# Batch 0's start rearranged and batch 2's attention moved three slots, in a banded-attention and low-rank mixer kernel

## Chip, cores, metric

One NeuronCore of a Trainium2 chip. The metric is the device time of one execution in microseconds (us), median of several. A profile's span (first to last instruction) is some 1.7 us shorter than the execution that it belongs to.

## The reference

```python
# attention: q, k, v are (8 batches, 8 heads, 576, 64), float32
scores = scale * q @ k.T                      # per batch and head
mask   = (0 <= i - j) & (i - j < 64)          # a band of 64
attn   = softmax(where(mask, scores, -1e9))
x      = (attn @ v) as (8, 576, 512)
# mixer
u   = x + (x.T @ U @ V).T                     # U (576, 32), V (32, 576)
out = u + relu(u @ w_ch1) @ w_ch2             # 512 -> 2048 -> 512
```

The 8 x 576 rows are worked on in nine chunks of 512 rows for the two large products. The attention of batch b+1 is slipped into the product of chunk b.

## The kernel before

A chunk is 32 slots. Slots 0 to 15 are each four matmuls of 512 columns and a relu (`ch1`), slots 16 to 31 four matmuls into the output (`ch2`). Pieces of the next batch's attention are put behind given slots:

```python
PLACE_2 = {                      # batch 2, inside chunk 1
    "S": [5, 5, 8, 8, 10],       # scores, exponential, mask
    "PV": [13, 13, 15, 15, 17],  # attention times V
    "TX": [12, 13, 14, 15, 16],  # DMA transposes of batch 3's K and Q
    "U": [19], "V": [21, 22, 23], "UT": [23, 24, 25, 26, 27],
}
```

Batch 0 has no product to hide in. It stands alone at the start, with matmuls whose result nobody reads (`unread`, `idle`) to keep TensorE busy. Its mask is added by a matmul of the identity with a bias (`masked`) instead of a product on DVE:

```python
def turn_over(n, cols=CH):                     # CH = 512
    for _ in range(n):
        nc.tensor.matmul(unread[:, 0:cols], idle[:, 0:P], idle[:, 0:cols], start=True, stop=True)

turn_over(9)
# ... masks ...
for what in ("K0", "K1", "Q0", "Q1", "S0", "S1", "K2", "K3", "Q2", "Q3", "S2", "S3"):
    # K, Q: 12 transposes into PSUM and a copy; S: bias matmuls, scores, exponential
    # ... cut ...
    turn_over({"K1": 3, "Q1": 1, "S0": 1, "K3": 1, "Q3": 1}.get(what, 0))
a["S"][HP]()                                   # the last block of all heads
# ... cut ...
for t in range(NT + 2):
    if t < NT:
        a["PV"][t]()                           # value tile t
    if 2 <= t < NFULL + 2:
        a["XT"][t - 2](); a["U"][t - 2]()
    elif t < 2:
        a["idle"](2)                           # two unread matmuls
for f in [a["U"][NT - 1]] + a["X3"] + a["HT"]:
    f()
# then chunk 0
```

All loads of K, Q, V and the weights stand in one queue of GpSimd, in this order: batch 0's K, Q, V, `w_ch1`, batch 1's K, Q, V, `w_ch2` in four parts, batch 2's K and Q. DMA transposes and the stores of the output stand in SyncE's.

The softmax here doesn't subtract the row's maximum and nothing guards it: scores larger than these inputs give would overflow.

## Time and profile before

| | |
|---|---|
| time | 330.74 us, median of 3 (330.69 to 330.99) |
| TensorE busy | 312.7 of 329.0 us |
| first product of chunk 0 | 26.39 us |
| PE waits at batch 2's scores | 2.67 us, until 73.67 |
| DMA engines busy (mean of 16) | 90% or more in slices 2 to 21 of 40, to 173 us |

In a timeline line the columns are start, length, engine, source line, operation, output and inputs, and in brackets how long the engine was idle before it and what ended that. "issue" means that no event of the program explains it.

### The profile page before, as it was taken

What the parts mean: (1) busy time and instruction counts of PE and PEld (TensorE: products, weight loads), DVE (VectorE), ACT (ScalarE), POOL (GpSimd) and SP (SyncE); (2) the same over time, 40 slices, a digit from 0 to 9 for tenths busy, and PEclk for the clock granted to TensorE, in tenths of its full rate; (3) what the DMA queues carried; (4) which work ended last, traced back from release to release, by engine and by line L of the source; (5) the groups of instructions that cost most, each with busy time, mean ns of one, the idle gap of its engine ahead of it and who ended that gap; (6) DMA issues with size and microseconds to landing.
All of it is one profiled execution on the core that took longest, in us unless ns stands there. A gap on an engine that the chain in (4) does not pass through costs nothing.

```text
span 329.0 us, 6715 instructions
## 1 busy us (share of the span) xinstructions
PE 312.7 (95%) x2790; PEld 147.0 (45%) x2790; DVE 171.2 (52%) x313; ACT 95.9 (29%) x150; POOL 103.0 (31%) x134
## 2 busy tenths in 40 slices
PE   6889999969999999899999999999999999999995
PEld 2544544534454444444444444444444444444442
DVE  4555486238645854476537653865387425114211
ACT  2515650317223330154016400640054001301400
POOL 8771778636537755407800400000000000000000
PEclk9979999999999999999999999999999999999999
DMA  8999999999999999999994796244200330021011
GB/s 114 156 220 197 161 193 166 124 173 173 138 147 211 166 143 146 187 181 149 157 175 101 103 119 176 54 89 104 90 26 2 79 99 32 0 82 48 0 66 64
DMA packets 151871, 39.56 MB, mean 120 GB/s; under 512 B 140960, under 2 KB 146080, under 8 KB 151840
## 3 DMA queue, kind: packets, MB, share of 16 engines
q0 software_dynamic: 100096, 18.36, 80.5%
q1 hardware_dynamic: 51744, 20.77, 35.0%
q8 instruction: 22, 0.36, 0.5%
q14 instruction: 9, 0.07, 0.1%
HBM read 37.14 MB, written 9.44 MB: 142 GB/s over the span
## 4 chain that ended last, share of the span: by engine, by line
PE 77%; DMA 9%; DVE 6%; ACT 5%; issue 1%; SPq 1%; POOL 0%; ACTq 0%; POOLq 0%
PE psA L583 32%; PE psU L605 32%; ACT pts L334 4%; PE xr L389 4%; DMA qf<-qn_110 2%; DMA uTc<-un 2%; DMA vA_104<-in_v_dram 2%; PE sc L315 2%; PE psv L506 2%; DMA qg<-in_q_dram 2%; DVE pts L336 2%; PE pshh L432 1%; DVE un L519 1%; PE uam L464 1%; SPq L284 1%
## 5 line engine op out<-in xcount | busy, mean ns | idle before, releaser
L583 PE MATMUL psA<-uTc,w1b 128*128 128x512 bf16 x576 | 132.0, 379 | 4.4 <-DMA uTc<-un 1.1
L583 PEld LDWEIGHTS <-w1b 128*128 128x128 bf16 x576 | 54.1, 98 | 68.3 <-issue 5.1
L614 DVE TENSOR_TENSOR osb<-psU,un 128x512 f32<-128x512 f32 x36 | 24.8, 690 | 79.3 <-PE psU L605 79.3
L334 ACT ACTIVATE pts<-sc 128x1024 bf16<-128x1024 f32 x32 | 31.4, 1028 | 7.7 <-PE sc L315 7.3
L336 DVE TENSOR_TENSOR pts<-pts,maskA 128x1024 bf16<-128x1024 bf16 x28 | 19.6, 703 | 11.4 <-ACT pts L334 11.4
L135 POOL DMA_DIRECT2D vA_105<-in_v_dram x16 | 14.1, 893 | 29.3 <-PE one L389 25.1
L519 DVE TENSOR_TENSOR un<-psv,xs_103 128x512 bf16<-128x512 f32 (+1 forms) x20 | 13.1, 686 | 11.7 <-PE psv L506 11.6
L519 DVE TENSOR_TENSOR un<-psv,xs_102 128x512 bf16<-128x512 f32 (+1 forms) x20 | 13.0, 684 | 11.0 <-PE psv L506 11.0
L135 POOL DMA_DIRECT2D vA_104<-in_v_dram x16 | 14.2, 894 | 14.0 <-PE xr L389 7.4
L126 POOL DMA_DIRECT2D qn_110<-in_q_dram x15 | 12.7, 847 | 10.8 <-DMA vA_105<-in_v_dram 4.7
L389 PEld LDWEIGHTS <-pts 128*64 128x64 bf16 x512 | 11.1, 113 | 10.7 <-issue 5.8
L126 POOL DMA_DIRECT2D kn_108<-in_k_dram x15 | 12.8, 851 | 9.5 <-DMA vA_105<-in_v_dram 5.2
L315 PEld LDWEIGHTS <-kf 64*64 64x64 bf16 x704 | 9.9, 107 | 10.9 <-issue 10.6
L126 POOL DMA_DIRECT2D kn_109<-in_k_dram x15 | 12.9, 860 | 5.9 <-DMA vA_104<-in_v_dram 3.7
L315 PE MATMUL sc<-qf,kf 64*64 64x128 bf16 (+1 forms) x576 | 11.3, 213 | 2.8 <-DMA qf<-qn_110 2.7
L126 POOL DMA_DIRECT2D qn_111<-in_q_dram x15 | 12.9, 859 | 3.1 <-DMA qn_111<-in_q_dram 1.3
L412 DVE TENSOR_TENSOR xs_102<-xr,rcp 128x512 bf16<-128x512 f32 (+1 forms) x18 | 12.4, 691 | 0.6
L506 PE MATMUL psv<-hh,vrep 128*128 128x512 bf16 x40 | 12.6, 379 | 0.0
L411 DVE RECIPROCAL rcp<-xr 128x8 f32<-128x8 f32 (+1 forms) x35 | 7.1, 202 | 10.3 <-PE xr L389 10.1
L412 DVE TENSOR_TENSOR xs_103<-xr,rcp 128x512 bf16<-128x512 f32 (+1 forms) x17 | 11.8, 692 | 0.6
L541 ACT COPY uTc<-tpu 128x512 bf16<-128x512 bf16 x9 | 5.3, 586 | 11.2 <-PE tpu L538 11.2
L389 PE MATMUL xr<-vA_104,pts 128*64 128x65 bf16 x160 | 6.6, 201 | 1.7 <-issue 1.4
(543 smaller groups left out, 514.7 us busy)
## 6 DMA issues: line engine op xcount, KB each, us to landing
out_dram<-osb SPq DMA_DIRECT2D x36, 256.0 KB, 4.1
vA_104<-in_v_dram POOLq DMA_DIRECT2D x16, 128.0 KB, 7.0
w1b<-in_moe_w_ch_dram POOLq DMA_DIRECT2D x2, 1024.0 KB, 16.0
vA_105<-in_v_dram POOLq DMA_DIRECT2D x16, 128.0 KB, 10.9
w2b<-in_moe_w_ch_dram POOLq DMA_DIRECT2D x4, 512.0 KB, 13.1
kn_108<-in_k_dram POOLq DMA_DIRECT2D x12, 128.0 KB, 11.8
qn_110<-in_q_dram POOLq DMA_DIRECT2D x12, 128.0 KB, 12.1
kn_109<-in_k_dram POOLq DMA_DIRECT2D x12, 128.0 KB, 8.6
```

The source lines that it names most:

```text
L126: nc.gpsimd.dma_start(out=dst[0:rows, t, :, :], in_=src[b, :, t * P : t * P + rows, :].rearrange("h p d -> p h d"),)
L135: nc.gpsimd.dma_start(out=va[:, t, :, 0:D], in_=v[b, :, t * P : (t + 1) * P, :].rearrange("h p d -> p h d"),)
L315: nc.tensor.matmul(sc[g][r0 : r0 + W, col * W : (col + n) * W], keys_of(j, u, rs), queries_of(j, blk, n, rs), start=not spare, stop=last o ...
L334: nc.scalar.activation(out=dst, in_=sc[:], func=ACT.Exp, scale=scale)
L336: nc.vector.tensor_tensor(out=dst, in0=dst, in1=maskA.rearrange("p g n w -> p g (n w)"), op=ALU.mult)
L389: nc.tensor.matmul(dst, pts[:, h // 2, h % 2, blk, :] if blk < NB - 1 else ptl[:, h // 2, h % 2, :], rhs, start=True, stop=True,)
L412: nc.vector.tensor_tensor(out=x[lo:hi, t, :, :].rearrange("p (a h) d -> p a h d", a=2), in0=xv[:, :, :, 0:D], in1=rcp[lo:hi].to_broadcast( ...
L506: nc.tensor.matmul(ps[0][:, n, :], vrep[:, off : off + P], hh["sb"][:], start=True, stop=True)
L519: nc.vector.tensor_tensor(out=u_tiles[g][rs, :], in0=ps[0][rs, n, :], in1=x[rs, t, :, :].rearrange("p h d -> p (h d)"), op=ALU.add,)
L583: nc.tensor.matmul(ps[:], w1b[:, dc, i * P : (i + 1) * P], uTc[:, :, dc, :], start=(dc == 0), stop=(dc == NDC - 1),)
L605: nc.tensor.matmul(acc[t][:], c1[i][:, t * P : (t + 1) * P], w2b[:, i, :], start=(i == 0), stop=(i == NFC - 1),)
L614: nc.vector.tensor_tensor(out=osb[:], in0=acc[t][:], in1=u_tiles[g][:], op=ALU.add)
```

## The change

Its intent is to shorten batch 0's start and to take the wait out of batch 2's scores. Five things are changed:

```diff
-turn_over(9)
+turn_over(56, 96)                                    # 56 unread matmuls of 96 columns
 # copies of K and Q of batch 0 out of PSUM
-copy = nc.vector.tensor_copy if spare and j >= HP // 2 else nc.scalar.copy      # K
+copy = nc.vector.tensor_copy if spare and j == 2 else nc.scalar.copy
-nc.vector.tensor_copy(out=place_of(qt, j), ...)                                 # Q
+copy = nc.scalar.copy if spare and j == 3 else nc.vector.tensor_copy
 # bias matmuls (B) are a piece of their own
-"K0 K1 Q0 Q1 S0 S1 K2 K3 Q2 Q3 S2 S3"
+"K0 K1 B0 B1 Q0 Q1 S0 S1 K2 K3 B2 Q2 B3 Q3 S2 S3 B4 S4"
-turn_over({"K1": 3, "Q1": 1, "S0": 1, "K3": 1, "Q3": 1}.get(what, 0))
+turn_over({"B1": 1, "Q1": 1, "S1": 1, "Q3": 1}.get(what, 0))
-        elif t < 2:
-            a["idle"](2)
+        elif t == 1:
+            a["idle"](1)
 PLACE_2
-    "S": [5, 5, 8, 8, 10], "PV": [13, 13, 15, 15, 17],
-    "U": [19], "V": [21, 22, 23], "UT": [23, 24, 25, 26, 27],
+    "S": [8, 8, 11, 11, 13], "PV": [16, 16, 18, 18, 20],
+    "U": [21], "V": [23, 24, 25], "UT": [25, 26, 27, 28, 29],
```

More of the change, by code (lines that the diff above doesn't have):

```diff
@@ L277, in f @@
             def f():
-                nc.vector.tensor_copy(out=place_of(qt, j), in_=tr(qb, j, b == 1))
+                copy = nc.scalar.copy if spare and j == 3 else nc.vector.tensor_copy
+                copy(out=place_of(qt, j), in_=tr(qb, j, b == 1))
             return f
@@ L302, in queries_of, with masked, SB @@
             return halves[rs, u0 : u0 + 2 * HP : 2 * HP - 1, :]
-        def masked(sc, bias):
+        sbank = {}
+        def masked(j):
+            sc = ps_big.tile([P, 2, CH], FP32, name="sc", tag="big")
             if spare:
+                bias, cols = maskB.rearrange("p n w -> p (n w)"), CH
+                if j == HP:
+                    bias, cols = maskB[:, 2:3, :].to_broadcast([P, HP, W]), HP * W
                 for g in range(2):
-                    nc.tensor.matmul(sc[:, g, :], ident[:], bias, start=True, stop=False)
+                    nc.tensor.matmul(sc[:, g, 0:cols], ident[:], bias, start=True, stop=False)
+            sbank[j] = sc
+        def SB(j):
+            return lambda: masked(j)
         def scores(sc, col, j, u, blk, n, last=False):
@@ L325, in f @@
             def f():
-                sc = ps_big.tile([P, 2, CH], FP32, name="sc", tag="big")
-                masked(sc, maskB.rearrange("p n w -> p (n w)"))
+                if j not in sbank:
+                    masked(j)
+                sc = sbank[j]
                 banks = [sc[:, g, :] for g in range(2)]
@@ L348, in SC8 @@
             else:
-                sc = ps_big.tile([P, 2, CH], FP32, name="sc8", tag="big")
+                if HP not in sbank:
+                    masked(HP)
+                sc = sbank[HP]
                 groups = [(sc, 0, 2)]
-                masked(sc[:, :, 0 : HP * W], maskB[:, 2:3, :].to_broadcast([P, HP, W]))
                 banks = [sc[:, g, :] for g in range(2)]
@@ L548, in attention @@
         pcs["S"] = [SC(j) for j in range(HP)]
+        pcs["B"] = [SB(j) for j in range(HP + 1)]
         pcs["S"].insert(0 if b >= NXU else HP, SC8)
@@ L641 @@
     PLACE_2 = {
-        "S": [5, 5, 8, 8, 10],
-        "PV": [13, 13, 15, 15, 17],
+        "S": [8, 8, 11, 11, 13],
+        "PV": [16, 16, 18, 18, 20],
         "TX": [12, 13, 14, 15, 16],
-        "U": [19],
-        "V": [21, 22, 23],
-        "UT": [23, 24, 25, 26, 27],
+        "U": [21],
+        "V": [23, 24, 25],
+        "UT": [25, 26, 27, 28, 29],
     }
@@ L684 @@
     )
-    for what in ("K0", "K1", "Q0", "Q1", "S0", "S1", "K2", "K3", "Q2", "Q3", "S2", "S3"):
+    order = "K0 K1 B0 B1 Q0 Q1 S0 S1 K2 K3 B2 Q2 B3 Q3 S2 S3 B4 S4"
+    for what in order.split():
         j = int(what[1])
-        if what[0] == "S":
-            a["S"][j]()
+        if what[0] in "SB":
+            a[what[0]][j]()
         else:
@@ L692 @@
             load_low_rank()
-        turn_over({"K1": 3, "Q1": 1, "S0": 1, "K3": 1, "Q3": 1}.get(what, 0))
-    a["S"][HP]()
+        turn_over({"B1": 1, "Q1": 1, "S1": 1, "Q3": 1}.get(what, 0))
     nc.vector.tensor_copy(out=maskA[:, 1, :, :], in_=maskA[:, 0, :, :])
```

## The prediction

> **What bounds the kernel now.** I read the page first. TensorE (PE) is busy 95% of the span, and in the forty slices it falls below 9 only in the first four slices and in slice nine. Each slice is 8.2 us.
>
> ```profile
> PE   6889999969999999899999999999999999999995
> PEclk9979999999999999999999999999999999999999
> ```
>
> From about 74 us to the end PE runs nearly without a break: listing every PE idle time with its cause gives only one wait of 1.1 us and pairs of 0.2 and 0.4 us per chunk. So the change, which touches only batch 0 and batch 2's slots, can win in two places: the first 26 us and the gap near 72 us. I then read the PE timeline of both.
>
> ```profile
> 68.82 1.89 PE L583 MATMUL psA<-uTc,w1b 128*128 128x512 bf16 x8
> 70.64 0.35 PE L315 MATMUL sc<-qf,kf 64*64 64x128 bf16 x12
> 73.67 0.50 PE L315 MATMUL sc<-qf,kf 64*64 64x128 bf16 x24 [2.67 <-DMA qf<-qn_110]
> ...
> 136.70 1.90 PE L583 MATMUL psA<-uTc,w1b 128*128 128x512 bf16 x8 [1.07 <-DMA uTc<-un]
> ```
>
> Batch 2's scores stand in slot 5, start at 70.64, run 12 matmuls on data that is there, and then PE waits 2.67 us for a transposed tile of Q which lands at 73.62. That is gap B.
>
> ```profile
> 14.94 0.38 PE L309 MATMUL sc_410<-maskB,ident 128*128 128x256 bf16 x2 [0.23 <-ACT pts L334]
> 15.25 0.32 PE L315 MATMUL sc_410<-qf,kf 64*64 64x64 bf16 x16
> 15.86 0.39 PE L389 MATMUL xr<-vA_104,pts 128*64 128x65 bf16 x13 [0.29 <-ACT pts L334]
> 17.65 0.23 PE L389 MATMUL xr<-vA_104,pts 128*64 128x65 bf16 x3 [1.41 <-issue]
> 17.81 1.02 PE L464 MATMUL uam<-idle 128*128 128x512 bf16 x2
> ...
> 26.39 1.02 PE L583 MATMUL psA<-uTc,w1b 128*128 128x512 bf16 x4 [0.45 <-DVE uTc L493]
> ```
>
> In the start (gap A) 13 of the 16 matmuls of the first value tile run, and then PE stands for 1.41 us with nothing in the program to wait for. The page's DMA part names an instruction queue with 22 packets and 0.36 MB, so 16 KB each; the trace's records of it put the first packet at 13.87 to 16.10 us, the second at 24.13 to 25.06. The stall falls at row 447 or 448 of PE's program, and 5,580 rows in 22 packets are 254 rows each. I take the stall for a late instruction block. The windows view shows what follows:
>
> ```profile
> 14.44:17.86 3.42, 1.49 (x53) 1.10 (x46) 0.06 (x1) 2.07 (x4) 2.95 (x5) 1.00 1.22 175
> 17.86:21.27 3.42, 3.42 (x41) 1.47 (x39) 2.03 (x6) 0.67 (x1) 3.42 (x5) 0.50 1.22 217
> ```
>
> The columns are length, then busy time of PE, PEld, DVE, ACT and POOL, then the granted clock. In a stretch with 1.49 of 3.42 us busy the clock was 1.00; in the next one it is 0.50.
>
> [...]the half-clock record is 3.413 us long, and 512-column matmuls start 0.43 us apart before 4.2 us and 0.216 after.[...]
>
> **The change, part by part.**
>
> *Batch 2's slots, 5 to 8, 8 to 11, 10 to 13.* Nothing is added. A slot is four 512-column matmuls at 0.216 us, so 0.86 us; three are 2.6 us of ready work put ahead of the wait. PE would reach the scores at 70.64 + 2.60 = 73.24, run its 12 ready matmuls (0.25) and wait from 73.49 to 73.62, were the rest unchanged. Gain about 2.5 us, less what an earlier start takes back below. At the new slots DVE has two V shifts (1.3 us), two mask products (0.69 each) and a relu after two exponentials of 1.03; with three buffers for the product I count the relu done about when PE wants the buffer, so at most 0.3 us is lost.
>
> *56 short matmuls for 9 long.* At half clock 96 columns take about 80 ns (half the speed of the 0.216 us per 512 warm); from 1.26 to 4.2 us some 37 run, the other 19 at 43 ns end at 5.1. K lands at 6.39 (first transposes at 6.43), so they delay nothing. What they do is to add 94 rows ahead: the listing of the order puts row 448 now in the middle of the fourth score block[...].
>
> *Bias matmuls ahead of Q.* Four of 0.216 and one filler replace three fillers: from 7.06 they end at 8.15 while Q landed at 7.88, so Q's transposes start 0.3 us later, Q0's copy ends at 9.5 instead of 9.17, the first exponential starts at 10.0 for 9.78. The second scores need no bias any more, so this is all it costs.
>
> *Copies of K3 and Q3 on ACT.* DVE did K2, K3, Q2, Q3 from 11.26 to 14.01 in a row; now K2 and Q2 end near 13.3, and ACT does K3 and Q3 between the exponentials, to about 14.0. The third exponential starts at 14.1 (13.87 before). No gain on the path; it is bound by Q2, whose data lands at 11.05 and whose copy is behind K2's.
>
> *Value tiles.* So the first of them starts at about 16.1 (15.86 before). But without the stall, at full clock, and with one filler of 0.22 for four that took 2.05 us, the five are paced by DVE: 0.21 + 0.69 with gaps 0.95 us each. DVE would be done at 16.5 + 5 x 0.95 = 21.3 instead of 24.01. From there to the first product took 2.4 us; chunk 0 would start at 23.7 instead of 26.39. Up to 2.7 us.
>
> *Sum and what is taken back.* 2.7 + 2.5 = 5.2 us if all comes through. But DMA runs full and most loads do not move with PE: the landings that the trace records are 23.22 for the first half of w1b, 34.69 for batch 1's Q (PE wanted it at 36.47, slack 1.78) and 49.65 for the last quarter of w2b (issued at 35.71, the longest of the four below; wanted at 51.29, slack 1.64).
>
> ```profile
> 34.98 1.48 POOL L225 DMA_DIRECT2D w2b<-in_moe_w_ch_dram  x2 [2.56 <-DMA qg<-in_q_dram]
> ...
> DMA to landing us min/median/max: 12.1/13.1/13.9
> ...
> 51.29 0.39 PE L605 MATMUL psU<-w2b,c_12_831 128*128 128x512 bf16 x1
> ```
>
> These loads are issued as earlier loads land (the bracket: an older load released this one), not as PE advances. So of the 2.7 at most about 1.6 passes 51 us, and with a block or a cold window left over perhaps 1.2; I count 1.4. At batch 2's scores PE then comes at 73.24 - 1.4 = 71.8, and the tile of Q, whose transposes start behind the first output store (53.09, which moves with PE), may come about 1 us earlier, at 72.6: the wait left is 72.6 - 72.05 = about 0.5 after the ready matmuls. Gap B gives 2.67 - 0.5, some 2.2. Behind that everything is PE's own pace: the wait of 1.07 at 136.70 follows from SyncE's row of transposes, which starts with PE, so I keep it. Sum 1.4 + 2.2 = 3.6; 330.74 - 3.6 = 327.1, of which I make 327.0.
>
> **The rivals.** *The start gives nothing.* The block stall moves into the scores and[...] comes again ahead of chunk 0: block 2 took its packet at 24.13, 6.5 us after row 448 was passed at 17.65[...]. Then only gap B is closed: about 328.2. *Everything passes.* If the loads move along with the earlier start, 2.7 + 2.5, and if the 1.07 at 136.70 goes too, 6.3: 324.5 to 325.5. The loads' latencies of 12 to 18 us on full queues speak against it. *The transposes become the bound again.* With batch 2 later in its chunk and PE 3.6 earlier, batch 3's transposed Q (landing at 99.25, wanted in slot 1 of the next chunk at 104.1) keeps 104.1 - 3.6 - 99.25 = 1.2 us; its issue starts when batch 2's fourth scores are done, at about the same time as before. If that is eaten, a wait of under 1 us comes back in chunk 2, and the wait at 136.70 can grow by as much: 328 to 329. *Slower:* for that ACT and DVE at slots 8 to 13 would have to stop PE for over 3 us; batches 3 to 7, with scores in slots 1 and 4, lose 0.6 us a chunk to the same conflict. I see no way to it.
>
> **Range and chances.** The first two rivals span 324.5 to 328.2, the third adds up to 1 us. The start carries most of the doubt (0 to 2.7), gap B less (1.5 to 2.7). Range 325.6 to 328.8. Over 2% faster means under 324.1, 6.6 us: more than both parts in full, so 4%. Slower by 2%: under 1%.
>
> **What would show it.** Right: no PE wait over 0.6 us at batch 2's scores; first product of chunk 0 between 23.5 and 25.2; clock 1.00 from 14 to 22 us; the "issue" gap gone from the value tiles, and found, if at all, in the fourth scores; waits of a few tenths at batch 1's Q or the last quarter of w2b near 50 us. Wrong: a half-clock record in the first 26 us, an issue gap of over 1 us ahead of chunk 0, a wait on DMA of over 1 us between 26 and 52 us or in chunk 2. The prediction fails upward if the loads issued in the first 20 us land earlier too, because then nothing takes the start's gain back.

## The result

327.44 us, median of 4 (326.82 to 329.19), against 330.87 (4 runs). The ratio is 0.9893, interval 0.9845 to 0.9941: faster by 1.1%, clear of noise, and inside the range predicted. A ratio here is the mean time of one kernel's fast runs over that of the other's of the same rounds, so it is not quite the ratio of the medians that are quoted.

From the page of the changed kernel, PE's busy tenths and the granted clock in 40 slices:

```profile
PE   7789899999999999899999999999999999999995
PEclk9999999999999999999999999999999999999999
```

The weak slice nine has gone, and so has the 7 in the clock's row. The PE timeline of the changed kernel at the places that the prediction showed for the one before:

```profile
14.76 0.36 PE L326 MATMUL sc<-qf,kf 64*64 64x128 bf16 x13 [0.31 <-issue]
15.23 0.38 PE L316 MATMUL sc<-maskB,ident 128*128 128x256 bf16 x2
15.54 0.32 PE L326 MATMUL sc<-qf,kf 64*64 64x64 bf16 x16
16.25 0.45 PE L402 MATMUL xr<-vA,pts 128*64 128x65 bf16 x16 [0.39 <-ACT pts L346]
...
23.54 1.02 PE L597 MATMUL psA<-uTc,w1b 128*128 128x512 bf16 x4 [0.45 <-DVE uTc L506]
...
35.06 0.45 PE L262 MATMUL tpw<-ident,qg 96*64 96x96 bf16 x12 [1.27 <-DMA qg<-in_q_dram]
...
72.19 0.50 PE L326 MATMUL sc<-qf,kf 64*64 64x128 bf16 x24 [0.25 <-DMA qf<-qn]
...
132.82 1.47 PE L597 MATMUL psA<-uTc,w1b 128*128 128x512 bf16 x6 [1.26 <-DMA uTc<-un]
```

All 16 matmuls of the first value tile run in one piece. The "issue" gap is in the fourth scores and 0.31 us long. Chunk 0 starts 2.85 us earlier, at 23.54. At 35.06 a wait of 1.27 us has come that was not there before: batch 1's Q lands at 35.01, where it landed at 34.69 before. At batch 2's scores 0.25 us of waiting is left of 2.67. The span is 325.1 us for 329.0. These 3.9 us divide as follows: 2.42 at batch 2's scores, 0.19 lost at the wait near 132 (1.26 for 1.07), and so some 1.65 won in the start: 2.85 at chunk 0, less the new wait of 1.27 and small differences. Up to the span's last us the trace records the granted clock in stretches: 13.65 us full, 3.41 half and 307.20 full in the kernel before, 317.44 full here. These are 4, 1, 90 and 93 times 3.413 us; a window here is that long, counted from the edge of a stretch. The windows view, in the columns of the prediction, for two windows of this run's clock; in the kernel before, the windows at this place began at 14.44 and 17.86, and the clock was half in the second:

```profile
13.56:16.97 3.41, 2.36 (x84) 1.73 (x86) 0.21 (x1) 3.30 (x5) 2.08 (x4) 1.00 1.73 170
16.97:20.38 3.41, 2.78 (x65) 1.92 (x60) 3.27 (x8) 0.62 (x1) 3.29 (x6) 1.00 1.21 228
```

PE is busy 2.36 us of 3.41 in the first (69%; 1.49 before, 44%), and the clock stays at 1.00.

### The profile page after: what moved, and what is told of

It is laid out like the page before. It is cut to its first block, busy times and chain, and to the rows that moved or that the text cites.

```text
span 325.1 us, 6773 instructions
## 1 busy us (share of the span) xinstructions
PE 309.4 (95%) x2806; PEld 149.9 (46%) x2831; DVE 169.7 (52%) x311; ACT 96.8 (30%) x152; POOL 104.1 (32%) x134
## 4 chain that ended last, share of the span: by engine, by line
PE 73%; DMA 12%; DVE 4%; ACT 4%; POOL 2%; SPq 2%; issue 1%; POOLq 0%; ACTq 0%
PE psU L619 33%; PE psA L597 30%; DMA qg<-in_q_dram 5%; ACT pts L346 3%; PE xr L402 3%; DMA vA<-in_v_dram 3%; DMA uTc<-un 3%; PE sc L326 2%; DMA qf<-qn 2%; PE psv L519 2%; SPq L285 1%; DVE pts L348 1%; PE pshh L445 1%; DVE c L606 1%; DVE un L532 1%
## 5 line engine op out<-in xcount | busy, mean ns | idle before, releaser
L619 PE MATMUL psU<-w2b,c 128*128 128x512 bf16 x556 | 130.4, 379 | 1.2 <-issue 0.2
L608 ACT ACTIVATE c<-psA 128x512 bf16<-128x512 f32 x75 | 44.7, 598 | 167.8 <-PE psA L597 167.8
L619 PEld LDWEIGHTS <-c 128*128 128x128 bf16 x576 | 54.9, 98 | 65.8 <-issue 3.0
L606 DVE TENSOR_SCALAR c<-psA 128x512 bf16<-128x512 f32 x69 | 46.0, 686 | 20.7 <-PE psA L597 20.0
L135 POOL DMA_DIRECT2D vA<-in_v_dram x32 | 28.5, 898 | 25.6 <-PE one L402 12.9
L532 DVE TENSOR_TENSOR un<-psv,xs 128x512 bf16<-128x512 f32 (+1 forms) x40 | 25.9, 684 | 20.6 <-PE psv L519 20.4
L126 POOL DMA_DIRECT2D kn<-in_k_dram x30 | 25.9, 864 | 26.1 <-DMA vA<-in_v_dram 14.2
L126 POOL DMA_DIRECT2D qn<-in_q_dram x30 | 25.3, 845 | 13.8 <-DMA vA<-in_v_dram 5.7
L425 DVE TENSOR_TENSOR xs<-xr,rcp 128x512 bf16<-128x512 f32 (+1 forms) x35 | 24.2, 691 | 1.2
L402 PE MATMUL xr<-vA,pts 128*64 128x65 bf16 x296 | 12.2, 196 | 0.6 <-ACT pts L346 0.4
```

Of the source, the lines that this page charges most:

```text
L126: nc.gpsimd.dma_start(out=dst[0:rows, t, :, :], in_=src[b, :, t * P : t * P + rows, :].rearrange("h p d -> p h d"),)
L135: nc.gpsimd.dma_start(out=va[:, t, :, 0:D], in_=v[b, :, t * P : (t + 1) * P, :].rearrange("h p d -> p h d"),)
L402: nc.tensor.matmul(dst, pts[:, h // 2, h % 2, blk, :] if blk < NB - 1 else ptl[:, h // 2, h % 2, :], rhs, start=True, stop=True,)
L425: nc.vector.tensor_tensor(out=x[lo:hi, t, :, :].rearrange("p (a h) d -> p a h d", a=2), in0=xv[:, :, :, 0:D], in1=rcp[lo:hi].to_broadcast( ...
L532: nc.vector.tensor_tensor(out=u_tiles[g][rs, :], in0=ps[0][rs, n, :], in1=x[rs, t, :, :].rearrange("p h d -> p (h d)"), op=ALU.add,)
L606: nc.vector.tensor_relu(out=c1[i][:], in_=ps[:])
```

## The experiments

Twelve kernels ran, in three series of four. Each series has its own 11 runs of the kernel before beside it; the first two series ran on one chip, the third on another. All results were correct. One run of after_again, 332.30, counts as slow (over 1.5% above its fastest) and is left out of its ratio. "chunk 0" is the start of its first product in the profiled run, and the two waits are PE's at batch 2's scores and at the chunk that starts near 132 to 139 us.

| kernel | median us (lowest to highest) | before | ratio (95%) | chunk 0 | wait, batch 2 | wait near 132 |
|---|---|---|---|---|---|---|
| e1_slots_only | 328.33 (326.02 to 328.96) | 332.03 | 0.9873 (0.9834 to 0.9912) | 27.87 | 0.34 | none |
| e2_start_only | 332.00 (331.53 to 335.05) | 332.03 | 1.0004 (0.9961 to 1.0047) | 23.80 | 0.71 + 2.49 | 1.90 |
| e3_long_fillers | 328.09 (326.54 to 329.14) | 332.03 | 0.9870 (0.9829 to 0.9911) | 26.86 | 0.21 | 0.64 |
| e4_late_start | 326.35 (325.47 to 328.05) | 332.03 | 0.9825 (0.9788 to 0.9863) | 25.09 | none | 0.28 |
| after_again | 327.27 (326.85 to 332.30) | 331.61 | 0.9865 (0.9839 to 0.9892) | 23.54 | 0.17 | 1.34 |
| e9_eleven_long | 329.39 (328.27 to 332.25) | 331.61 | 0.9941 (0.9904 to 0.9977) | 27.70 | none | 1.53 |
| e10_tiny_fillers | 328.65 (327.25 to 329.76) | 331.61 | 0.9907 (0.9875 to 0.9939) | 25.15 | none | 2.54 |
| e5_fill_and_slots | 326.52 (326.16 to 327.05) | 331.61 | 0.9844 (0.9817 to 0.9871) | 24.37 | 0.94 | 0.52 |
| e6_copies_back | 327.14, one run | 331.35 | - | 23.55 | 0.81 | 0.9 |
| e7_bias_back | 327.21, one run | 331.35 | - | 23.88 | 0.81 | 0.6 |
| e8_late_masks | 324.91 (323.57 to 327.66) | 331.35 | 0.9813 (0.9771 to 0.9855) | 23.85 | 1.00 | 1.85 |
| e11_masks_and_ut | 322.62 (322.23 to 324.66) | 331.35 | 0.9745 (0.9712 to 0.9779) | 23.84 | 1.77 | 0.60 |

The kernel before spreads far more than its first three runs showed: 329.55 to 334.06 over the first two series. The granted clock says part of why. One window of 3.41 us at half clock lowers a run's mean clock by 0.5 x 3.41 / 330 = 0.005, and of its 33 runs 18 have 0.990 or less, so the worth of two such windows or more (the half clock at the very end of a span counts too: the profile shown for the kernel before has one window and 0.5 us of that, and 0.994). Those take 332.8 us on average in the first series, against 331.1 for the others; 332.7 against 331.2 in the second; 332.1 against 330.9 in the third. Runs at 0.995 and more still spread from 329.55 to 332.11, so the clock is not all of it. A single profile shows only one draw.

### Slots alone

```diff
 # kernel before, and only:
-    "S": [5, 5, 8, 8, 10],  ...
+    "S": [8, 8, 11, 11, 13], ...          # the whole new PLACE_2
```

> Kernel before with batch 2's slots alone. Theory (the slots close gap B by themselves, the start is separate): chunk 0's first product at 26.4 us as before, wait at batch 2's scores 0.1 to 0.4 us instead of 2.67, no new PE wait over 0.3 us in slots 8 to 20, time 2.3 to 2.6 us under before, 328.2 to 328.5. Rival (the later slots make ACT and DVE stop PE): waits on DVE or ACT of over 0.5 us in chunk 1, gain under 1.8 us.

The wait shrank to 0.34 us and none came in slots 8 to 20, as the theory had it. But the median fell by 3.7 us, not by 2.3 to 2.6: in the medians the slots alone are worth as much as the whole change (0.9873, against 0.9893 and 0.9865 for the changed kernel). In its profiled run 2.33 us of the wait are gone, and the wait near 132 too (1.07 before), against a start that is 1.48 us later; what made the rest of the median's fall is not shown. This profiled run had a slower start, as its PE timeline tells:

```profile
6.23 0.69 PE L262 MATMUL tpg<-ident,kg 96*64 96x96 bf16 x12 [0.95 <-DMA kg<-in_k_dram]
...
19.22 0.23 PE L389 MATMUL xr<-vA,pts 128*64 128x65 bf16 x3 [1.56 <-issue]
...
75.06 0.50 PE L315 MATMUL sc<-qf,kf 64*64 64x128 bf16 x24 [0.34 <-DMA qf<-qn]
```

The 12 transposes took 0.69 us where the kernel before's profile has 0.45: half clock. The trace's clock record is full only from 10.17 us here, and half again from 20.41 to 23.82. The start thus differs between the two profiled runs, by 1.48 us at chunk 0, with the same instructions.

### Start alone

```diff
 # kernel after, and only PLACE_2 as it was:
-    "S": [8, 8, 11, 11, 13], ...
+    "S": [5, 5, 8, 8, 10],  ...
```

> Kernel after with batch 2's old slots. Theory (the landing of the transposed Q tile sets the pace, and moves only about as far as the first output store does): chunk 0 at 23.5, wait at batch 1's Q about 1.3, wait at batch 2's scores again 2.4 to 2.9, tile landing near 72.1, time about 1.5 us under before, 329.3. Rival A (the start passes in full): 2.8 us under before, 328.0. Rival B (the tile does not move at all, the start is worth nothing): wait over 4 us, 330.8.

The tile landed at 72.5 us, 1.1 earlier than in the profile on record, and the wait was 3.2 us in two parts, somewhat over what the theory said (2.4 to 2.9). The time said otherwise: 332.00 against 332.03, nothing gained. Its PE timeline, the window of its clock with the wait and the one behind it, and two later ones that are taken up below:

```profile
69.83 0.25 PE L326 MATMUL sc<-qf,kf 64*64 64x128 bf16 x4 [0.71 <-DMA qf<-qn]
72.57 0.50 PE L326 MATMUL sc<-qf,kf 64*64 64x128 bf16 x24 [2.49 <-DMA qf<-qn]
73.00 4.45 PE L597 MATMUL psA<-uTc,w1b 128*128 128x512 bf16 x12
```

```profile
70.06:73.48 3.42, 0.93 (x30) 0.61 (x27) 0.00 (x0) 0.60 (x1) 1.44 (x3) 1.00 1.69 198
73.48:76.89 3.41, 3.41 (x10) 1.21 (x9) 2.66 (x4) 1.34 (x2) 0.99 (x2) 0.50 1.63 198
134.92:138.33 3.41, 1.51 (x8) 0.51 (x6) 1.95 (x3) 0.00 (x0) 0.69 (x1) 1.00 1.49 196
138.33:141.75 3.42, 3.42 (x65) 1.73 (x64) 1.12 (x2) 2.02 (x4) 0.68 (x1) 1.00 1.58 222
```

PE was busy 0.93 of 3.42 us, and the clock then went to half for 3.41 us: twelve products took 4.45 us where the same twelve behind the wait of the kernel before took 2.76. So here the wait cost its length and, in the half-clock window behind it, 1.7 us more. Against the profile of the kernel before the sum closes: 1.10 us earlier behind the wait, 1.69 lost at half clock, 0.83 more at the next wait on DMA (1.90 for 1.07) make 1.42 us more, and the spans are 330.4 and 329.0. Whether the earlier start has a part in the clock's fall is not shown. Neither rival A nor the theory's 329.3 held. Of rival B it held that the start is worth nothing here, but the tile did move.

The last two window lines are a warning: PE was busy for 1.51 us, about as little as the 1.49 of the window from 14.44 us in the kernel before, and here the clock stayed full. In these two the busy time alone does not tell whether the clock falls.

### A later start on purpose

```diff
 # kernel after, and:
+    a["idle"](6)                          # 24 unread matmuls of 128 columns, 1.3 us
     for f in [a["U"][NT - 1]] + a["X3"] + a["HT"]:
         f()
```

> Kernel after with 24 more idle matmuls of 128 columns (1.3 us at full clock) ahead of the last part of batch 0, same result. Theory (loads that do not move with PE take back 1.3 us at batch 1's Q): chunk 0 at 24.8, the wait at batch 1's Q gone or under 0.2, time within 0.3 us of after. Rival (the start counts in full): 1.3 us slower than after.

```profile
25.09 1.02 PE L597 MATMUL psA<-uTc,w1b 128*128 128x512 bf16 x4 [0.44 <-DVE uTc L506]
...
34.90 0.45 PE L262 MATMUL tpg<-ident,kg 96*64 96x96 bf16 x12
35.18 0.42 PE L262 MATMUL tpw<-ident,qg 96*64 96x96 bf16 x12
...
71.67 0.65 PE L326 MATMUL sc<-qf,kf 64*64 64x128 bf16 x36
```

Chunk 0 starts 1.55 us later than in the changed kernel; K and Q of batch 1 are transposed with no wait between them, as Q has landed (at 34.90; at 35.01 in the changed kernel); and the time is 326.35, not over that of the changed kernel on the same chip in the next series (327.27). The last 1.3 us that the start wins are worth nothing: the rival that counts them in full would be at a ratio of some 0.990, and the interval ends at 0.986. In the traces Q lands at 34.61 in e1, with chunk 0 at 27.87, and at 35.01 in the changed kernel, with chunk 0 at 23.54: this load does not move with PE. That e4 came out 0.9 us lower fits the wait near 132 us, 0.28 for 1.34 in the profiled runs. Against e1, the slots alone in the same series, it is 2.0 us lower.

### What the 56 short matmuls do: rows or columns

Three kernels differ from the changed one in the first fillers alone.

```diff
-turn_over(56, 96)
+turn_over(9)                              # e3: as before, 4608 columns, 94 rows fewer
+turn_over(10); turn_over(1, 256)          # e9: the same 5376 columns, 90 rows fewer
+turn_over(56, 32)                         # e10: the same rows, a third of the columns
```

> Kernel after with the 9 long fillers of before, so 94 rows fewer ahead of everything. Theory (a late instruction block stalls PE at row 448, wherever that row stands, and loads take back what the start wins beyond 1.3 us): the issue gap comes back in the second value tile, 0.7 to 1.5 us long, chunk 0 at 24.2 to 25, wait at batch 1's Q shrinks to 0 to 0.6, time within 0.4 us of after; if the clock falls to half behind the gap, up to 1 us more. Rival (the stall is not tied to the row but to the first value tile or its data): a gap at the first value tile again. Rival (the start counts in full): about 1.2 us slower than after.

> Kernel after with 10 fillers of 512 columns and one of 256: the same 5376 columns as 56 of 96, but 90 rows fewer. It parts the two things that the short fillers do. Theory (rows move the late instruction block, columns keep PE busy up to K): fillers end near 5.8 us, clock full by 7 us in all or nearly all executions, but the issue gap of 0.7 to 1.5 us back at the second value tile and with it, in some executions, a half-clock window near 18 to 21 us; chunk 0 at 24.3 to 26; time 0 to 0.8 us over after. Rival (only the length matters): no gap, chunk 0 at 23.5.

> Kernel after with 56 fillers of 32 columns: the same rows as after, a third of the columns. Theory: fillers end near 3 us, PE idle 3 us before K[...] and the transposes and first scores run at half clock; the issue gap stays in the fourth scores, under 0.6 us; chunk 0 at 24.3 to 25.5; time 0 to 0.8 us over after since batch 1's Q takes back up to 1.3 us. Rival (only the rows matter): as after, 23.5.

The unaltered kernel ran beside e9 and e10 as their yardstick.

> The changed kernel unaltered, as the yardstick on this chip. By the runs so far: 326.4 to 327.5, one in four or five executions about 1.7 us slower[...].

It gave 327.27 us, one of six runs at 332.30 with a mean clock of 0.985. The PE timelines of e3 and of e9 at the gap:

```profile
19.16 0.19 PE L402 MATMUL xr<-vB,pts 128*64 128x65 bf16 x1 [1.22 <-issue]
```

```profile
18.68 0.22 PE L402 MATMUL xr<-vA,pts 128*64 128x65 bf16 x2 [1.47 <-issue]
```

In e3 the gap stands ahead of the first matmul of the second value tile, in e9 ahead of the 15th of the first tile (the expectation named the second tile; counting the rows, of which each matmul has two, its weight load and itself, gives the 15th of the first: 4 rows, so two matmuls, ahead of e3's). Both are row 448 of PE's weight loads and matmuls in order of time. So are the gaps of the kernel before, of e1, of the changed kernel, e2, e4 and e8, and, shown below, of e5 and e7 (445 to 448, as some records are missing). In these ten kernels it is the row and not the work that fixes the place. The 16 KB packet of the instruction queue ends 1.3 to 2.0 us ahead of the resumption in these traces (for instance 16.10 and 17.65 in the kernel before; 17.85 and 19.16 in e3; 12.93 and 14.76 in the changed kernel). In e10 PE comes to that row only at 15.9, 2.5 us behind the packet's end (13.45), and there is no gap. That the packet is what PE waits for is inferred from this; no record says so. e3's chunk 0 at 26.86 missed its 24.2 to 25: the clock was full only from 9.45 us, and half again from 19.69 to 23.10, behind the gap.

The windows view of e9 shows what follows the gap, and that of e10, whose gap stays hidden, something else further on:

```profile
15.73:19.14 3.41, 1.50 (x51) 1.13 (x50) 0.20 (x1) 1.71 (x4) 2.73 (x5) 1.00 1.17 228
19.14:22.55 3.41, 3.08 (x41) 1.68 (x40) 2.65 (x8) 0.67 (x1) 3.41 (x5) 0.50 1.24 218
22.55:25.97 3.42, 3.42 (x23) 1.61 (x22) 1.53 (x3) 0.18 (x1) 1.75 (x3) 0.50 1.20 215
```

```profile
131.45:134.87 3.42, 0.88 (x6) 0.41 (x5) 2.04 (x3) 0.00 (x0) 1.42 (x2) 1.00 1.54 187
134.87:138.28 3.41, 3.41 (x58) 1.65 (x57) 1.11 (x2) 1.71 (x4) 1.20 (x2) 0.50 1.40 269
```

In e9 the clock was full from 5.49 us, as was expected (by 7 us), but behind the window of the gap, with 1.50 us busy, it was half for two windows: chunk 0 at 27.70, 329.39 us. All six of its runs have mean clocks of 0.985 to 0.990. In e10 there is no issue gap of note, but PE stood idle for 3.46 us ahead of K, the clock was full only from 11.99 us, and chunk 0 came at 25.15; 328.65 us. So in the start both halves of "many" and "short" work: the rows move the gap into the fourth scores, where it is 0.31 us long (1.22 in e3, 1.47 in e9), the columns keep PE busy until K lands (its wait for K is 0.33 us, for 3.46 in e10). What of this reaches the end differs. The same stop of PE near 104 us, in the unaltered kernel, in e9 and in e10:

```profile
104.10 2.75 PE L597 MATMUL psA<-uTc,w1b 128*128 128x512 bf16 x12 [0.18 <-DVE c L606]
```

```profile
106.37 0.59 PE L597 MATMUL psA<-uTc,w1b 128*128 128x512 bf16 x2 [0.18 <-DVE c L606]
```

```profile
104.07 2.75 PE L597 MATMUL psA<-uTc,w1b 128*128 128x512 bf16 x12 [0.18 <-DVE c L606]
```

e9 is 2.27 us behind there and 2.45 at the end, so losing the rows costs time. e10 is not behind at all: its later start has been taken up, as in e4. Its profiled run lost its 2.7 us (span 327.8 for 325.1) near 134 us, where PE waited 2.54 us for 1.34 and the clock then went to half once. Its median is 1.4 us over the unaltered kernel's, over the 0 to 0.8 expected as e9's 2.1 is, but that the missing columns are the cause is not shown.

### Fillers and slots without the rest

```diff
 # kernel before, and only:
-turn_over(9)
+turn_over(56, 96)
+# and the new PLACE_2; bias matmuls, copies, idle turns as before
```

> Kernel before with the 56 short fillers and batch 2's new slots only; bias matmuls, copies and idle turns as before. Theory (those other parts do not reach the end, batch 1's Q takes back what they win): issue gap in the fourth scores, chunk 0 at 23.9 to 24.6, wait at batch 1's Q 0.3 to 0.9, time within 0.4 us of after. Rival (bias and copies are worth something): 0.7 us or more over after.

```profile
15.29 0.42 PE L315 MATMUL sc<-qf,kf 64*64 64x64 bf16 x16 [0.62 <-issue]
...
24.37 1.02 PE L583 MATMUL psA<-uTc,w1b 128*128 128x512 bf16 x4 [0.44 <-DVE uTc L493]
35.39 0.45 PE L262 MATMUL tpw<-ident,qg 96*64 96x96 bf16 x12 [0.77 <-DMA qg<-in_q_dram]
```

326.52 us, 0.75 under the changed kernel beside it, where within 0.4 was expected. The other parts of the change win nothing at the end, and this has the lowest median of the versions that contain only parts of the change. In the profiled runs it is 1.03 us behind the unaltered kernel near 104 us, and the next wait on DMA, 0.52 for 1.34, gives 0.82 of that back.

```diff
 # e6: kernel after, copies of K3 and Q3 back on DVE
 # e7: kernel after, each bias pair back beside its scores, 3 fillers ahead of Q
```

> Kernel after with the copies of K3 and Q3 back on DVE; one look, for the start only. Theory (the third exponential is bound by Q2's copy, which is behind K2's on DVE, so moving K3 and Q3 to ACT wins little): third exponential starts at 14.0 to 14.8 (14.16 in after), chunk 0 within 0.8 us of 23.5, wait at batch 1's Q takes the difference. Rival (the copies are what wins the start): chunk 0 at 24.8 or later.

> Kernel after with each bias pair back beside its scores, fillers ahead of Q again 3; one look, for the start only. Theory (the bias matmuls ahead of Q cost 0.3 us at the first exponential and are worth nothing later): first exponential near 9.8 (10.04 in after), chunk 0 within 0.5 us of 23.5. Rival (bias early is what wins the start): chunk 0 at 24.3 or later.

In e6 the third exponential started at 13.87 (14.16 in the changed kernel) and PE was through with batch 0 early enough to wait 0.85 us at 23.55 for the first half of `w_ch1`: with the copies back the start is not slower, and it meets the landing of the weights. In e7 the first exponential began at 9.64 (10.04), the gap was 0.74 us, chunk 0 at 23.88. Both as the theory said; one run each, 327.14 and 327.21.

### What else the page offered

The waits of the changed kernel name ten stops of PE for relus on DVE, 2.9 us in all, in batches 3 to 7. This is no part of the change.

```diff
 # e8: DVE's mask products of batches 3 to 7 become pieces of their own
+    "M": [3, 3, 3, 6, 6],                 # scores and exponentials stay in [1, 1, 1, 4, 4]
 # e11: e8, and one tile of batch 3's u, the third, transposed by TensorE
-                if b >= NXU:
+                if b >= NXU and not (b == NXU and t == 2):
                     nc.sync.dma_start_transpose(out=dst, in_=u_tiles[g][:])
+    PLACE_3 = {**PLACE, "UT": [18, 18, 22, 19, 20]}
```

> Not a test of the prediction but of the 0.6 us a chunk that the page shows for batches 3 to 7: kernel after with DVE's mask products of batches 3 to 7 issued two slots after their scores instead of ahead of the next relus. If PE waits there because DVE, in order, holds a relu behind a product that waits for an exponential, the ten waits on DVE's relus (2.9 us) go and the time falls by 2.3 to 2.9, to 324.4 to 325. Rival (the waits are the throughput of DVE): they move to another slot, time within 0.5 us of after.

> The kernel of late masks with one of batch 3's transposes of u, the last one that the next chunk waits for, done by TensorE (four matmuls, 0.22 us) instead of by DMA. If the PE wait of 0.3 to 2.5 us near 132 us is that transfer's landing, it is gone and the time falls by another 0.6 to 1.3 us against late masks alone, with a narrower spread: 323.3 to 324.2. Rival (another tile's landing takes its place): wait of over 0.5 us there, time as late masks alone.

All PE waits from 100 us on that the view lists, of the changed kernel and then of e8:

```profile
PE psA L597 <- DVE c L606: 2.9, 10, 0.4
PE psA L597 <- DMA uTc<-un: 1.3, 1, 1.3
```

```profile
PE psA L610 <- DMA uTc<-un: 1.9, 1, 1.9
```

The ten stops, 2.9 us, are gone: it was the order on DVE, where a relu stood behind a product that waited for an exponential, not DVE's throughput. e8 ran at 324.91, e11 at 322.62. The wait near 132 fell to 0.60 in e11 and did not vanish, so another tile's landing is next, as the rival had it, though not its time; the range of its runs was 2.4 us, and the gain of 2.3 over e8 is more than that wait can explain, so what e11's part is worth alone is not settled. Against the kernel before e11 is at 0.9745 and is the fastest that ran.

## Why the prediction was right

*Where the time could come from.* It named two places, the start and the wait at batch 2's scores. Those are the two places in which the traces differ. Right. It misread the page in one point: slice 17 is an 8 as well, and it holds the wait of 1.07 at 136.70, which later decided much.

*Gap B closes.* It said that 2.6 us of ready work covers the wait and that 0.5 is left, the tile landing at 72.6. Measured 0.25, and 72.15. Right, and so is the term "Gap B gives 2.67 - 0.5, some 2.2" for the two profiles: 2.42. In the medians the slots alone gave 3.7 us, in a series in which the kernel before ran at 332.03. What the prediction left out is a half clock behind such a wait. In e2's trace it is there, for 3.41 us, and cost 1.7 us more; that the kernel before has the same thing in many of its runs is inferred from their mean clock, not from a trace.

*The start.* Chunk 0 at 23.7 was said, 23.54 measured. The first value tile at 16.1: 16.25. DVE done with the tiles at 21.3: 21.16. Full clock over 14 to 22 us: yes. Bias matmuls costing 0.3 at the first exponential: 10.04 for 9.78. Copies without gain: e6. The stall was to lie, if anywhere, in the fourth scores: PE went on there at 14.76, after 0.31 us. The place is right. What sets a packet's time is not shown: it starts with PE at row 347 (before) and 344 (after), some 100 rows ahead of the stop, and when it was asked for is not recorded. Packets are not 254 rows each by 5,580 / 22, as the first 447 rows needed none of the 22; from the first start to the last PE runs 246 rows a packet. The second packet came at 18.66 to 19.60 us (24.13 to 25.06 before), and the rival's second stall ahead of chunk 0 did not come.

*What the fillers do.* "What they do is to add 94 rows ahead" is half of it for the start. e10 has the rows, and its clock was full only from 11.99 us, with chunk 0 at 25.15: their length matters there as well, though it is not shown to reach the end. Their end was put at 5.1 us and measured at 5.3 to 5.9, since the moment at which the clock rises (4.2 in the profile read) was 4.4 to 6.7 in the kernels with these fillers.

*What loads take back.* A cap of about 1.6 us was said: the last quarter of `w_ch2` was wanted at 49.65 for 51.29, 1.64 us earlier, and landed at 49.21, so no wait was left there. e4 confirms the mechanism: 1.3 us more work in the start, no time lost. Right. But one sign was set wrongly: "a few tenths" of waiting at batch 1's Q stood under right, "over 1 us between 26 and 52" under wrong, and the wait was 1.27. The prediction's own cap, at most 1.6 of 2.7 us past 51 us, needs over 1 us of waiting by then; the sign contradicts the cap, and the cap was right.

*The start's share of 1.4 us.* In the two profiles it is some 1.65. In the medians it is not settled: alone the start was worth nothing (e2); behind the new slots the changed kernel's ratio is that of the slots alone within the noise, while e4 is 2.0 us under e1 in one series. The two parts do not add, and the slots must come first.

*The wait at 136.70.* "I keep it" fits in size for the changed kernel (1.26), and was wrong in its reason. It was said to follow PE's pace; over the twelve kernels it is 0 to 2.5 us, by when a transposed tile lands. In the profiled runs this decided some of the order among kernels that differ by under 1 us.

*The total.* 3.6 us was the sum; 3.4 was measured in the first series and 4.3 in another. Some of this closeness is luck: the kernel before runs anywhere from 329.55 to 334.06, and the prediction started from three runs of 330.7 to 331.0.

## What to carry to other kernels

A wait that nobody can shorten is best covered with ready work before anything upstream is made faster: bringing PE to it earlier only made it longer here (3.2 us for 2.67 in e2). If a stall has no waiter and stays at the same row of the program when the work around it changes, count rows: here it stayed at row 445 to 448 in ten kernels, and a packet of the instruction queue ended 1.3 to 2.0 us before PE went on. And where half-clock windows come and go between executions, one profile is one draw: look at the mean clock of every run before a difference of 1 us is explained, and look in the trace where a difference arises, as e10's did 130 us behind its edit.

## What the traces leave open

- What lowers the clock. Windows with 1.49, 1.50, 1.57 and 1.61 of 3.41 us busy (before, e9, e1, e3), with mostly narrow matmuls and a longest gap of 1.22 to 1.56 us, were followed by half clock. One with 2.36 (69%, the changed kernel) was not, but neither was one of 1.51 with a gap of 1.90 us (e2, wide matmuls only). So neither one gap nor the busy time decided; what did stays open.
- What raises it. In e9 a half-clock window with 3.08 of 3.41 us busy, mostly narrow matmuls, was followed by another at half clock; that one, with 3.42 busy, was followed by full clock. In the changed kernel a window with 3.08 busy (3.32 to 6.73 us) was followed by full clock. In what busy is counted stays open.
- Where the instruction packets come in. In a start whose score matmuls follow one another every 20 ns (18 in 0.36 us) PE stopped for 0.3 to 1.6 us near row 448 (445 to 448 in the records), in ten kernels. The first packet of the span started in these kernels with PE at row 344 to 388 and ended 12.9 to 17.8 us into the span, with loads of 12 to 18 us latency beside it; PE resumed 1.3 to 2.0 us after. What sets these times is not shown.
